# A gated recurrence and a gated convolution on one core: loads per 1024-token chunk, squares of both channel halves together, and a new order of all queues

## Chip, cores and metric

The kernel runs on one core of one Trainium2 chip. The metric is the device time of one execution in microseconds. The engines are TensorE (PE in the profile, its weight loads PEld), VectorE (DVE), ScalarE (ACT) and GpSimd (POOL); SyncE (SP) only issues transfers.

## What is computed

Two layers in a row, for x, r_gate and i_gate of 4 x 6336 x 256 (batch, time, channel), all float32:

```
a    = exp(8 * sigmoid(r_gate) * log(clip(sigmoid(a_param))))
u    = sqrt(max(1 - a*a, 1e-6)) * sigmoid(i_gate) * x
y[t] = a[t] * y[t-1] + u[t]                         # along time, from 0 in each batch
gate = sigmoid(sum over k of conv_w[k] * y[t-4+k])  # causal, 5 taps, per channel
out  = (gate * (y @ w_val)) @ w_out
```

## The kernel before

The 25344 tokens lie in one row. They are cut into 28 chunks: 0 and 1 of 256 tokens, 2 of 512, 3 to 25 of 1024, 26 of 512 and 27 of 256. A chunk of 1024 consists of two windows of 512; there are 51 windows. The 256 channels are two halves h of 128.

The order is written out by hand in ORDER, a string of words such as `ex.5.0` or `cv.7@0,1` (name, chunk or window, half, PSUM banks). The words are emitted in that order, and each engine works through its own words strictly in sequence, waiting for what its next word needs. The steps:

- `lr`, `li`, `lx` (L292, SP): load a window of r, i or x; each partition gets J consecutive tokens of 256 channels (J = 4: 4 KB). The rings have four window slots each; a load waits until the engine that read the slot's old content is done.
- `ta`, `tb` (L310, L313, ScalarE): tanh of half the r and i gates of a whole chunk (sigmoid = half of one plus tanh), to bf16.
- `tr` (L357, TensorE): transposes of the r side, so that channels lie on partitions; `ex` (L378, ScalarE): Exp to a, in the order of time. From chunk 3 on most `tr`/`ex` cover two neighbouring chunks (GROUPS), so `ex.3.0` covers chunks 3 and 4.
- `sq` (L386, GpSimd): a*a per chunk and half; `sa` (L394) is the same on ScalarE, used for two of them (sa.25.1 and sa.27.1).
- `rt` (L405, ScalarE): square roots of 1 - a*a for one of 12 batches of chunks (BATCHES: [0], [1], [2], [3, 4], [5, 6, 7], ..., [23, 24, 25], [26, 27]), to bf16. Sqrt and Exp/Tanh are in different tables of ScalarE; where the next word needs the other table, a table load (L562) is put in.
- `pp` (L320, GpSimd): one plus tanh; `up` (L332, GpSimd): times x, giving the input of a window with bf16 channels laid in pairs of tokens. For windows 1, 2 and 6 `xp` and `uv` (L337, L346) do it on TensorE and VectorE.
- `nt` (L420, TensorE): the roots of a chunk back to tokens on partitions, as pairs of bf16 read as float32; `xg` (L450, VectorE): roots times input; `xt` (L461, TensorE): that product to channels on partitions. For chunks 26 and 27 the order is turned round (L435, L446).
- `sc` (L483, VectorE): the recurrence along time for one half of a chunk.
- `cv` (L495, TensorE): the convolution of a window as 20 small matmuls; `tg` (L502, ScalarE): its tanh; `vl` (L510, TensorE): y @ w_val; `gv` (L515, VectorE): gate times value.
- `ou` (L525, TensorE): times w_out; `cd` (L533, VectorE) or `ca` (L535, ScalarE): copy out of PSUM; `st` (L546, SP): store of the window.
- `wm` (L364): groups of five matmuls on TensorE whose result is not used.
- `s_kt` computes khf, the scale of Exp, from a_param through small operations on TensorE (L233), VectorE (L234 to L248) and ScalarE (L237); `s_diag` makes the matrices of the convolution, `s_wl` and `s_wcast` load and cast the weights.

Of the kernel before, what the change touches and what calls it, by code (L numbers as in the profile page):

```python
# [9 lines left out]
P = 128  # L10
# [14 lines left out]
NU = 8  # L25
# [13 lines left out]
s_ident s_small s_kt s_diag lr.2 lr.0 s_wl.3 lr.1 li.0 lr.3 s_wl.2 ta.2 ta.0 lr.4 tr.0.1@0 tr.2.0@1 lr.6 ta.1 lr.5  # L39
tr.1.0@2 tb.0 tr.0.0@3 li.1 tr.2.1@4 ex.2.0 li.2 tr.1.1@5 li.3 ex.1.1 lx.0 ex.0.1 sq.1.1 li.4 ex.1.0 sq.2.0 ex.0.0  # L40
ex.2.1 sq.1.0 ta.3 sq.2.1 pp.0 sq.0.0 sq.0.1 ta.4 tb.1 lr.10 tr.3.0@4,5 tb.2 lr.9 lr.8 lr.7 lx.2 tr.3.1@2,3 ex.3.0
s_wl.1 up.0 lx.1 lx.4 wm.10@6 ex.3.1 sq.3.0 wm.5@6 lx.3 wm.3@6 tb.3 sq.3.1 wm.9@6 wm.6@6 ta.6 pp.4 sq.4.1 ta.5 lr.13
li.5 xp.2@2,3 li.6 sq.4.0 li.7 lr.14 tr.5.0@4,5 lx.6 uv.2 pp.3 rt.0 rt.2 nt.0@0 up.4 xg.0 rt.1 xt.0@0,1 xp.1@2 rt.3
sc.0.0 nt.1@3 up.3 lx.5 nt.2@0 uv.1 s_wl.0 xg.1 xg.2 xt.1@2,3 sc.0.1 lx.7 sc.1.0 nt.3@6,7 lr.12 sc.1.1 xg.3 ex.5.0
xt.2@0,1 sc.2.1 sc.2.0 tb.4 cv.0@2,3 tr.5.1@4,5 xt.3@6,7 lr.11 li.8 sq.5.0 ex.5.1 tg.0 sc.3.0 pp.5 sc.3.1 cv.2@0,1
s_wcast cv.1@4,5 ta.8 xp.6@2,3 uv.6 vl.0@6,7 tg.1 tg.2 vl.2@0,1 up.5 ta.7 sq.6.1 lx.8 li.9 li.10 lr.17 lr.18
nt.4@2,3 gv.0 tb.5 tr.7.0@6,7 ou.0.0@4 gv.2 ex.7.0 xg.4 sq.6.0 cd.0.0 tr.7.1@0,1 sq.5.1 vl.1@2,3 ou.2.0@4,5 ex.7.1
gv.1 xt.4@6,7 ou.1.0@2 lx.9 li.12 cv.4@0,1 cd.2.0 cv.3@4,5 pp.7 sq.7.1 tb.6 pp.8 sq.7.0 tg.4 tg.3 rt.4 sc.4.1 st.0
sc.4.0 li.11 lr.15 lr.16 st.2 up.7 pp.9 li.14 li.13 vl.3@0,1 vl.4@4,5 gv.3 gv.4 cd.1.0 ou.3.0@0,1 pp.10 up.8 sq.8.1
# [57 lines left out]
def kernel(  # L107
# [82 lines left out]
    with tc.manual_schedule():  # L190
# [403 lines left out]
```

## Time and profile before

| | |
|---|---|
| median of three runs | 287.52 us (287.51 to 288.32) |
| span of the profiled execution | 286.4 us |
| what the median has beyond that span | 1.1 us |
| transfers | 104.76 MB, mean 366 GB/s |
| granted TensorE clock | 0.999 of full speed |

The profiled execution's own whole time is not listed apart from its span. A row of an engine's group reads: line, engine, operation, output and inputs with partitions x elements, count, busy time in us and mean ns of one, and the idle time before them with what ended it. A row of the timeline begins with its start and its length in us; a bracket gives the idle time before it. A row of the chain has a start and a length.

### The profile page before, as it was taken

To read this page: it belongs to the slowest core of one execution; us is meant where nothing else is said; L and a number is where in the kernel's file an instruction comes from. 1 tells how busy PE (TensorE), PEld (TensorE's weight loads), DVE (VectorE), ACT (ScalarE), POOL (GpSimd) and SP (SyncE) were. 2 spreads that over 40 slices of the span, in tenths; PEclk is the share of its full clock that TensorE was granted. 3 is DMA by queue.
4 is the path that set the end of the run, shared out by engine and by line. 5 is a ranking of instruction groups with operands and counts; after the bars stand their busy time and mean duration, and the time that the engine had idled before them with its cause. 6 is when DMAs were issued, how large, how long until landed. Compare 5 with 4: busy or idle time off the path is not lost.

```text
span 286.4 us, 6382 instructions
## 1 busy us (share of the span) xinstructions
PE 251.8 (88%) x2552; PEld 171.1 (60%) x2576; DVE 246.8 (86%) x214; ACT 273.6 (96%) x198; POOL 241.6 (84%) x161
## 2 busy tenths in 40 slices
PE   1387778899999999988988999989989899999993
PEld 1253447456656767455756676656646774767562
DVE  4002898969999899999999999999999999999991
ACT  5999999999999999999999999999999999898984
POOL 1659589899999999999999999999996999874600
PEclk9999999999999999999999999999999999999999
DMA  7999999999999999999999999999999999994536
GB/s 243 384 373 407 409 403 408 388 366 376 410 408 366 418 367 392 414 410 334 405 364 413 411 332 356 420 416 419 415 401 333 359 416 406 364 356 170 192 150 256
DMA packets 29996, 104.76 MB, mean 366 GB/s; under 512 B 3335, under 2 KB 3854, under 8 KB 29966
## 3 DMA queue, kind: packets, MB, share of 16 engines
q1 hardware_dynamic: 29952, 104.35, 94.5%
q8 instruction: 20, 0.33, 0.5%
q14 instruction: 10, 0.08, 0.1%
q10 hardware_dynamic: 14, 0.01, 0.0%
HBM read 78.39 MB, written 25.95 MB: 364 GB/s over the span
## 4 chain that ended last, share of the span: by engine, by line
ACT 33%; PE 29%; DVE 14%; issue 12%; DMA 8%; SPq 1%; ACTq 0%; DVEq 0%
ACT ering L405 8%; PE banks L495 8%; DVE yring L483 7%; PE banks L525 7%; DMA rring<-in_r_gate_dram 6%; ACT tgring L502 6%; ACT taring L310 5%; ACT tbring L313 5%; ACT aring L378 5%; PE banks L510 5%; PE banks L461 3%; DVE tgring L515 3%; PE banks L420 3%; ACT L562 3%; DVE oring L533 2%
## 5 line engine op out<-in xcount | busy, mean ns | idle before, releaser
L386 POOL TENSOR_TENSOR ering<-aring 128x1024 f32<-128x1024 f32 (+2 forms) x54 | 91.5, 1714 | 16.7 <-ACT aring L378 16.4
L332 POOL TENSOR_TENSOR uring<-tbring,xring 128x1024 bf16<-128x1024 bf16 (+1 forms) x48 | 101.1, 2119 | 3.6 <-DMA xring<-in_x_dram 3.1
L483 DVE TENSOR_TENSOR_SCAN yring<-aring,yring,banks 128x1024 bf16<-128x1024 f32 (+5 forms) x50 | 101.7, 2064 | 2.1 <-PE banks L461 1.9
L495 PE MATMUL banks<-yring,diag 64*64 64x512 bf16 (+7 forms) x1080 | 62.1, 361 | 2.3 <-ACT aring L378 1.6
L515 DVE SCALAR_TENSOR_TENSOR tgring<-tgring,banks 128x1024 bf16<-128x1024 bf16 (+1 forms) x51 | 59.1, 1178 | 4.0 <-PE banks L510 3.4
L320 POOL TENSOR_SCALAR tbring<-tbring 128x1024 bf16<-128x1024 bf16 (+1 forms) x48 | 49.1, 1032 | 6.8 <-ACT tbring L313 6.7
L378 ACT ACTIVATE aring<-banks,khf 128x2048 f32<-128x2048 bf16 (+3 forms) x38 | 54.2, 1476 | 0.4 <-PE banks L357 0.3
L525 PE MATMUL banks<-wo,tgring 128*128 128x256 bf16 x396 | 51.0, 274 | 3.7 <-DVE tgring L515 3.2
L502 ACT ACTIVATE tgring<-banks 128x1024 bf16<-128x1024 f32 (+1 forms) x51 | 50.2, 1011 | 2.0 <-PE banks L495 1.9
L510 PE MATMUL banks<-yring,wv 128*128 128x512 bf16 (+4 forms) x192 | 48.1, 359 | 3.7 <-ACT tgring L502 1.9
L310 ACT ACTIVATE taring<-rring 128x2048 bf16<-128x2048 f32 (+2 forms) x28 | 47.9, 1718 | 1.4 <-DMA rring<-in_r_gate_dram 1.4
L525 PEld LDWEIGHTS <-tgring 128*128 128x128 bf16 x396 | 41.2, 114 | 13.1 <-DVE tgring L515 8.8
L313 ACT ACTIVATE tbring<-iring 128x2048 bf16<-128x2048 f32 (+2 forms) x28 | 48.2, 1726 | 0.0
L405 ACT ACTIVATE ering<-ering 128x4096 bf16<-128x4096 f32 (+5 forms) x16 | 44.8, 2840 | 0.1
L495 PEld LDWEIGHTS <-diag 64*64 64x64 bf16 x1080 | 29.0, 106 | 25.6 <-issue 9.9
L533 DVE COPY oring<-banks 128x1024 f32<-128x1024 f32 (+1 forms) x36 | 41.9, 1182 | 1.4 <-PE banks L525 0.7
L357 PE MATMUL banks<-ident_b,taring 128*128 128x128 bf16 x396 | 29.9, 230 | 9.4 <-ACT taring L310 6.7
L357 PEld LDWEIGHTS <-taring 128*128 128x128 bf16 x396 | 26.5, 103 | 14.2 <-ACT taring L310 7.4
L510 PEld LDWEIGHTS <-wv 128*128 128x128 bf16 x216 | 19.7, 98 | 24.5 <-issue 10.3
L450 DVE TENSOR_TENSOR uring<-banks,uring 128x2048 bf16<-128x2048 bf16 (+2 forms) x26 | 29.4, 1134 | 3.5 <-PE banks L420 3.2
L420 PE MATMUL banks<-ident,ering 128*128 128x128 f32 x192 | 28.3, 289 | 1.1 <-ACT ering L405 0.9
L461 PE MATMUL banks<-ident,uring 128*128 128x128 f32 x192 | 25.9, 276 | 3.5 <-DVE uring L450 2.8
(49 smaller groups left out, 154.0 us busy)
## 6 DMA issues: line engine op xcount, KB each, us to landing
rring<-in_r_gate_dram SPq DMA_DIRECT2D x48, 512.0 KB, 8.2
iring<-in_i_gate_dram SPq DMA_DIRECT2D x48, 512.0 KB, 8.7
xring<-in_x_dram SPq DMA_DIRECT2D x48, 512.0 KB, 8.2
out_dram<-oring SPq DMA_DIRECT2D x48, 512.0 KB, 6.5
rring<-in_r_gate_dram SPq DMA_DIRECT2D x3, 256.0 KB, 4.1
iring<-in_i_gate_dram SPq DMA_DIRECT2D x3, 256.0 KB, 6.5
xring<-in_x_dram SPq DMA_DIRECT2D x3, 256.0 KB, 8.5
out_dram<-oring SPq DMA_DIRECT2D x3, 256.0 KB, 5.2
```

The source lines that it names most:

```text
L310: nc.scalar.activation(**tangent(c, taring, NTR, rring, NRI))
L313: nc.scalar.activation(**tangent(c, tbring, NTI, iring, NII))
L332: nc.gpsimd.tensor_tensor(out=u, in0=t1, in1=xt, op=ALU.mult)
L378: nc.scalar.activation(out=dst, in_=src, func=ACT.Exp, scale=khf[:, h:h + 1], bias=khf[:, h:h + 1])
L386: nc.gpsimd.tensor_tensor(out=e, in0=a, in1=a, op=ALU.mult)
L405: nc.scalar.activation(out=ering[:].bitcast(BF16)[:, 4 * o:4 * o + 2 * n], in_=ering[:, 2 * o:2 * o + 2 * n], func=ACT.Sqrt, scale=-0.25, ...
L483: nc.vector.tensor_tensor_scan(out=yring[:, h, col:col + o1 - o0], data0=aring[:, h, a_at[c] + o0:a_at[c] + o1], data1=xT[:, o0:o1], initi ...
L495: nc.tensor.matmul(out=gp[oh * 64:oh * 64 + 64, h, a:b], lhsT=diag[half * 64:half * 64 + 64, h, k, :], rhs=yring[half * 64:half * 64 + 64, ...
L502: nc.scalar.activation(out=tgring[:, w % NTG, :, 0:wins[w]], in_=live.pop(("gp", w))[:, :, 0:wins[w]], func=ACT.Tanh, scale=0.5)
L510: nc.tensor.matmul(out=val[:, m, a:b], lhsT=wv[:, hk, m * P:(m + 1) * P], rhs=yring[:, hk, col:col + b - a], start=(hk == 0), stop=(hk == ...
L515: nc.vector.scalar_tensor_tensor(out=tgring[:, w % NTG, :, 0:wins[w]], in0=tgring[:, w % NTG, :, 0:wins[w]], scalar=1.0, in1=live.pop(("va ...
L525: nc.tensor.matmul(out=ops[:, j * D:(j + 1) * D], lhsT=gv[:, hk, j:wins[w]:J], rhs=wo[:, hk, :], start=(hk == 0), stop=(hk == H - 1))
```

## The change

- ORDER is written anew for all engines. CHUNKS, BATCHES and GROUPS hold the same numbers as before.
- `lr`, `li` and `lx` load a whole chunk: one transfer of 1 MB for 1024 tokens, in which each partition gets eight consecutive tokens (8 KB). There are 28 loads of each kind instead of 51. x goes to slots numbered like those of the gates. Since partition p now holds tokens 8p to 8p + 7 of the chunk, `tr`, `ex`, `nt` and `xt` take steps over the chunk instead of over the window.
- `sq.c` without a half squares both halves of a chunk in one operation; chunks 0, 1, 2, 26 and 27 still have one per half. `sa`, and `sv`, which was not used, are gone.
- The bank of `s_kt` and `s_diag` is given in ORDER.
- Counted in ORDER: `sq` 54 to 33, `sa` 2 to 0, `ca` 15 to 17, `cd` 36 to 34, `wm` 17 to 10, loads 153 to 84. All other words have the same count. Changes between the Sqrt table and the other, 18 to 20.

The core of the diff:

```diff
-s_ident s_small s_kt s_diag lr.2 lr.0 s_wl.3 lr.1 li.0 lr.3 s_wl.2 ta.2 ta.0 lr.4 tr.0.1@0 tr.2.0@1 lr.6 ta.1 lr.5
-tr.1.0@2 tb.0 tr.0.0@3 li.1 tr.2.1@4 ex.2.0 li.2 tr.1.1@5 li.3 ex.1.1 lx.0 ex.0.1 sq.1.1 li.4 ex.1.0 sq.2.0 ex.0.0
-ex.2.1 sq.1.0 ta.3 sq.2.1 pp.0 sq.0.0 sq.0.1 ta.4 tb.1 lr.10 tr.3.0@4,5 tb.2 lr.9 lr.8 lr.7 lx.2 tr.3.1@2,3 ex.3.0
-s_wl.1 up.0 lx.1 lx.4 wm.10@6 ex.3.1 sq.3.0 wm.5@6 lx.3 wm.3@6 tb.3 sq.3.1 wm.9@6 wm.6@6 ta.6 pp.4 sq.4.1 ta.5 lr.13
-li.5 xp.2@2,3 li.6 sq.4.0 li.7 lr.14 tr.5.0@4,5 lx.6 uv.2 pp.3 rt.0 rt.2 nt.0@0 up.4 xg.0 rt.1 xt.0@0,1 xp.1@2 rt.3
...
-cv.41@0,1 st.33 gv.38 vl.37@6,7 lx.45 lr.50 st.35 cd.36.0 lx.46 ou.38.0@2,3 gv.37 li.47 rt.10 cv.40@4,5 tg.41
-ou.37.0@6,7 cd.38.0 nt.23@2,3 up.43 li.48 lr.49 st.36 cd.37.0 vl.41@6,7 xg.23 vl.40@0,1 up.45 gv.41 st.34 tg.40
-nt.24@2,3 xt.23@6,7 gv.40 up.46 xg.24 ou.39.0@0,1 cv.42@2,3 sc.23.0 ou.41.0@4,5 sc.23.1 tb.25 ca.39.0 ou.40.0@0,1
...
+s_ident lr.0 lr.2 lr.1 s_small li.1 ta.0 tr.0.1@5 tr.0.0@3 s_kt@0 wm.5@2 lr.3 s_wl.3 lx.1 li.0 ta.2 ta.1 tb.1 lx.0
+ex.0.1 li.2 lr.4 tr.2.1@2 tr.2.0@0 ex.2.0 tr.1.0@1 ex.1.0 tr.1.1@4 ex.2.1 ta.3 ex.1.1 ex.0.0 tb.0 sq.1.0 sq.2.1 sq.0.1
+sq.1.1 sq.0.0 xp.1@5 s_wl.2 lr.5 pp.0 sq.2.0 rt.0 rt.1 nt.0@6 nt.1@4 rt.2 lx.2 s_wl.1 s_wl.0 up.0 uv.1 xg.0 xt.0@3,0
+ta.4 xg.1 xt.1@2,1 tb.2 lr.6 tr.3.1@6,7 sc.0.0 ta.5 sc.0.1 sc.1.1 li.4 li.3 lx.3 s_diag@4 s_wcast ex.3.1 nt.2@5
+xp.2@0,1 uv.2 tr.3.0@3,4 ex.3.0 xg.2 xt.2@0,6 sc.1.0 cv.1@1,2 ta.6 sq.3 sq.4 cv.0@4,5 tg.0 sc.2.0 sc.2.1 vl.2@6,7
+cv.2@4,5 tg.1 tb.4 tg.2 tr.5.1@0,1 lr.8 lx.4 lr.7 vl.0@2,3 gv.0 tb.3 tr.5.0@4,5 gv.2 ou.0.0@7 ou.2.0@2,3 cd.0.0 cd.2.0
+ex.5.0 li.5 vl.1@2,3 li.6 rt.3 pp.5 pp.3 gv.1 up.3 pp.4 xp.6@2,3 uv.6 ou.1.0@4 cd.1.0 up.4 up.5 nt.3@6,7 xg.3 ta.8
+ex.5.1 sq.6 sq.5 nt.4@2,3 xg.4 xt.3@6,5 xt.4@7,4 wm.1@0 wm.8@1 ta.7 tr.7.1@2,3 st.0 st.2 st.1 lr.10 lx.5 lr.9 sc.3.1
+tb.5 ex.7.1 tr.7.0@0,1 sc.3.0 ex.7.0 cv.3@5,6 sc.4.1 sc.4.0 pp.8 sq.7 pp.7 cv.4@2,3 tg.4 tg.3 tb.6 vl.4@0,1 vl.3@6,7
+gv.3 gv.4 up.7 pp.9 up.8 ou.3.0@6,7 rt.4 cd.3.0 wm.6@3 ou.4.0@0,1 wm.3@2 vl.6@4,5 cv.6@2,3 lx.6 li.7 tg.6 st.3 li.8
...
+sc.21.0 tg.38 tr.25.0@0 ex.25.0 cv.37@5,6 tg.37 tr.25.1@3 ex.25.1 ou.36.0@0,1 xt.22@6,2 sc.21.1 cv.39@4,5 sc.22.1
+sc.22.0 vl.38@2,3 gv.38 pp.43 sq.25 tb.24 tg.39 ca.36.0 vl.37@4,5 rt.10 vl.39@6,7 cv.40@0,1 gv.39 gv.37 ou.38.0@2,3
+cv.41@6,7 cd.38.0 pp.45 pp.44 ou.37.0@4,5 cd.37.0 up.44 up.43 nt.23@2,3 xg.23 tg.40 li.26 st.36 st.33 li.27 lx.25
+st.37 st.38 vl.40@4,5 gv.40 tg.41 ta.26 vl.41@0,1 gv.41 ou.39.0@2,3 ca.39.0 tb.25 up.45 pp.46 up.46 xt.23@6,7 sc.23.0
...
-        def s_kt():
-            kps = banks[:, 0]
+        def s_kt(at):
+            kps = banks[:, at]
...
-        def load(w, which):
-            n = wins[w]
-            J = n // P
-            if which == "x":
-                dst = xring[:, w % NX, 0:J, :]
-            else:
-                ring = rring if which == "r" else iring
-                dst = ring[:, place(w, NRI if which == "r" else NII), 0:J, :]
-            nc.sync.dma_start(dst, flat[which][wstart[w]:wstart[w] + n, :].rearrange("(p j) d -> p j d", p=P))
-
-        def op_lr(w):
-            load(w, "r")
-
-        def op_li(w):
-            load(w, "i")
-
-        def op_lx(w):
-            load(w, "x")
+        def load(c, which):
+            w, k, n = cwins[c][0], len(cwins[c]), clen[c]
+            ring, slots = {"r": (rring, NRI), "i": (iring, NII), "x": (xring, NX)}[which]
+            at = place(w, slots)
+            dst = ring[:, at:at + k, 0:wins[w] // P, :].rearrange("p w j d -> p (w j) d")
+            nc.sync.dma_start(dst, flat[which][cstart[c]:cstart[c] + n, :].rearrange("(p j) d -> p j d", p=P))
+
+        def op_lr(c):
+            load(c, "r")
+
+        def op_li(c):
+            load(c, "i")
+
+        def op_lx(c):
+            load(c, "x")
...
         def op_tr(c, h, *at):
-            ws = [w for k in sorted(group_of[c], key=lambda k: a_at[k]) for w in cwins[k]]
-            J = wins[ws[0]] // P
+            cs = sorted(group_of[c], key=lambda k: a_at[k])
+            J = wins[cwins[c][0]] // P
             bank = banks[:, at[0]:at[-1] + 1].rearrange("c k n -> c (k n)").bitcast(BF16)
-            for g, w in enumerate(ws):
-                assert wins[w] == J * P
-                for j in range(J):
-                    o = (j * len(ws) + g) * P
-                    nc.tensor.transpose(out=bank[:, o:o + P],
-                                        in_=taring[:, place(w, NTR), j, h * P:(h + 1) * P],
-                                        identity=ident_b[:])
+            for g, k in enumerate(cs):
+                for v, w in enumerate(cwins[k]):
+                    assert wins[w] == J * P and len(cwins[k]) == len(cwins[c])
+                    for j in range(J):
+                        o = ((v * J + j) * len(cs) + g) * P
+                        nc.tensor.transpose(out=bank[:, o:o + P],
+                                            in_=taring[:, place(w, NTR), j, h * P:(h + 1) * P],
+                                            identity=ident_b[:])
             live["rT", c, h] = bank
...
-            J = wins[cwins[c][0]] // P
+            J = n // P
...
-        def op_sq(c, h):
-            e, a = squares(c, h)
+        def both_squares(c):
+            n = clen[c]
+            return (ering[:, H * e_at[c]:H * (e_at[c] + n)].rearrange("p (h n) -> p h n", h=H),
+                    aring[:, :, a_at[c]:a_at[c] + n])
+
+        def op_sq(c, *h):
+            e, a = squares(c, h[0]) if h else both_squares(c)
             nc.gpsimd.tensor_tensor(out=e, in0=a, in1=a, op=ALU.mult)
-
-        def op_sv(c, h):
-            e, a = squares(c, h)
-            nc.vector.tensor_tensor(out=e, in0=a, in1=a, op=ALU.mult)
-
-        def op_sa(c, h):
-            e, a = squares(c, h)
-            nc.scalar.activation(out=e, in_=a, func=ACT.Square)
 
...
         def op_nt(c, *at):
             bank = banks[:, at[0]:at[-1] + 1].rearrange("p b n -> p (b n)")
-            k = 0
-            for w in cwins[c]:
-                nq = wins[w] // (2 * P)
-                o = live["n", c] + (wstart[w] - cstart[c]) // 2
-                for q in range(nq):
-                    for h in range(H):
-                        e = o + h * clen[c] // 2
-                        nc.tensor.transpose(out=bank[:, k:k + P], in_=ering[:, e + q:e + wins[w] // 2:nq], identity=ident[:])
-                        k += P
+            k, n = 0, clen[c]
+            nq = n // (2 * P)
+            for q in range(nq):
+                for h in range(H):
+                    e = live["n", c] + h * n // 2
+                    nc.tensor.transpose(out=bank[:, k:k + P], in_=ering[:, e + q:e + n // 2:nq], identity=ident[:])
+                    k += P
             live["nT", c] = bank[:, 0:k]
...
+        def pairs(c):
+            return [(uring[:, (w + 1) % NU, q], v * (wins[w] // (2 * P)) + q)
+                    for v, w in enumerate(cwins[c]) for q in range(wins[w] // (2 * P))]
...
+            nq = clen[c] // (2 * P)
             for h in range(H):
                 bank = banks[:, at[h]]
-                for w in cwins[c]:
-                    nq = wins[w] // (2 * P)
-                    o = (wstart[w] - cstart[c]) // 2
-                    for q in range(nq):
-                        nc.tensor.transpose(
-                            out=bank[:, o + q:o + wins[w] // 2:nq],
-                            in_=uring[:, (w + 1) % NU, q, h * P:(h + 1) * P, :].rearrange("p d two -> p (d two)")
-                            .bitcast(FP32),
-                            identity=ident[:])
+                for u, q in pairs(c):
+                    nc.tensor.transpose(
+                        out=bank[:, q:clen[c] // 2:nq],
+                        in_=u[:, h * P:(h + 1) * P, :].rearrange("p d two -> p (d two)").bitcast(FP32),
+                        identity=ident[:])
                 live["xT", c, h] = bank
```

More of the change, by code (lines that the diff above doesn't have):

```diff
@@ L44 @@
[L44 to L48, printed above, removed]
@@ L327, in u_args @@
             return (uring[:, (w + 1) % NU, 0:wins[w] // (2 * P)].rearrange("p q d two -> p q two d"),
-                    by_pair(tbring[:, place(w, NTI)], w), by_pair(xring[:, w % NX], w))
+                    by_pair(tbring[:, place(w, NTI)], w), by_pair(xring[:, place(w, NX)], w))
         def op_up(w):
@@ L337, in op_xp @@
                 nc.tensor.matmul(out=ps[:, q], lhsT=ident[:],
-                                 rhs=xring[:, w % NX, 2 * q:2 * q + 2, :].rearrange("p two d -> p (two d)"),
+                                 rhs=xring[:, place(w, NX), 2 * q:2 * q + 2, :].rearrange("p two d -> p (two d)"),
                                  start=True, stop=True)
```

121 lines of the change are left out of this document (55 added, 66 removed).

## Prediction

> **What bounds the kernel now.** I read the page first, for its span and the engines' shares; then the busy time by stage; then the chain of waits, to see which engine ends each stage; then single rows for prices.
>
> ```profile
> span 286.4 us, 6382 instructions
> PE 251.8 (88%) x2552; PEld 171.1 (60%) x2576; DVE 246.8 (86%) x214; ACT 273.6 (96%) x198; POOL 241.6 (84%) x161
> ```
>
> ```profile
> 30.00:40.00 10.00, 7.48 (x87) 5.33 (x86) 9.39 (x11) 9.97 (x5) 5.77 (x5) 1.00 1.03 403
> 60.00:80.00 20.00, 18.96 (x182) 12.53 (x186) 17.89 (x13) 19.97 (x13) 20.00 (x12) 1.00 1.00 382
> 120.00:140.00 20.00, 18.01 (x172) 12.53 (x166) 19.62 (x16) 19.97 (x11) 20.00 (x13) 1.00 1.01 380
> 180.00:200.00 20.00, 18.85 (x197) 12.80 (x196) 19.80 (x16) 19.96 (x15) 19.92 (x13) 1.00 1.03 418
> 240.00:260.00 20.00, 19.56 (x183) 13.45 (x185) 19.68 (x16) 17.56 (x16) 15.53 (x10) 1.00 0.98 359
> ```
>
> A window row gives, after its length, the busy time of PE, weight loads, DVE, ACT and POOL, then granted clock, DMA share and GB/s. Every engine is nearly full, but from 30 to 240 us only ScalarE never pauses: 19.96 to 19.97 of 20. After 240 it has pauses (17.56) while TensorE is at 19.56. So there are three stages: a start, a middle that lasts as long as ScalarE's work, and a tail. The chain shows where the tail begins:
>
> ```profile
> 238.87 5.34 ACT ering L405
> 244.25 1.24 PE banks L420 x8
> 255.37 1.21 PE banks L495 x20
> 256.57 0.97 PE banks L510 x4
> 257.54 0.95 PE banks L420 x8
> 260.89 0.87 PE banks L525 x8
> 261.76 0.87 PE banks L461 x8
> 282.17 0.63 PE banks L525 x4
> 282.82 0.58 ACT oring L535
> ```
>
> The square roots of batch 10 (rt.10, L405) end at 244.2; nt.23 starts at once, and from there the chain is almost all TensorE up to 282.80. Then come the last copy and the store: 42.2 us from the end of rt.10 to the end of the span.
>
> So the sum has three terms: how much ScalarE work stands in its queue up to rt.10, how long ScalarE idles before it, and whether the 42.2 us change.
>
> **1. ScalarE's queue up to rt.10.** I count both orders. Each has 26 ta, 25 tb, 34 ex, 40 tg and 11 rt up to there, of the same sizes. Three things differ. The new order runs rt.0, rt.1 and rt.2 early, goes back to ta.4, and runs rt.3 later by itself: 18 table switches become 20, both new ones early. Copies on ScalarE (ca) up to there are 3 before and 5 after. The square sa.25.1 goes to GpSimd.
>
> ```profile
> 229.97 1.12 ACT L394 ACTIVATE ering<-aring 128x1024 f32<-128x1024 f32 x1
> 230.92 1.98 ACT L313 ACTIVATE tbring<-iring 128x2048 bf16<-128x2048 f32 x1
> 237.57 1.28 ACT L562 ACT_TABLE_LOAD   x1
> 238.87 5.33 ACT L405 ACTIVATE ering<-ering 128x6144 bf16<-128x6144 f32 x1
> 253.02 1.92 ACT L535 COPY oring<-banks 128x1024 f32<-128x1024 f32 x2
> 254.81 0.59 ACT L378 ACTIVATE aring<-banks,khf 128x256 f32<-128x256 bf16 x1
> ```
>
> From start to next start, a table load takes 1.30 us, a copy 0.90 (1.79 for two), the square 0.95. The term is 2 x 1.30 + 2 x 0.90 - 0.95 = **+3.5 us**. Nothing hides it, for ScalarE has no gap in the middle. The Exp (L378) now writes eight tokens per row instead of four, with the same element count, contiguous output and the same kind of stepped input: I take 0.
>
> **2. ScalarE's idle time at the start.**
>
> ```profile
> 0.71 1.28 ACT L191 ACT_TABLE_LOAD   x1 [0.71 <-PEq L578]
> 3.85 0.20 ACT L237 ACTIVATE ktmp<-ktmp 128x2 f32<-128x2 f32 x1 [1.85 <-DVE ktmp L236]
> 4.54 1.58 ACT L310 ACTIVATE taring<-rring 128x1024 bf16<-128x1024 f32 x2 [0.49 <-DMA rring<-in_r_gate_dram]
> 6.35 0.63 ACT L310 ACTIVATE taring<-rring 128x512 bf16<-128x512 f32 x1 [0.23 <-DMA rring<-in_r_gate_dram]
> 13.40 1.91 ACT L310 ACTIVATE taring<-rring 128x2048 bf16<-128x2048 f32 x1 [0.38 <-DMA rring<-in_r_gate_dram]
> ```
>
> ```profile
> 3.46 0.16 DVE L234 COPY ksig<-banks 128x2 f32<-128x2 f32 x1 [3.46 <-PE banks L233]
> ```
>
> The brackets give the wait before each row: 3.7 us so far, and a few smaller pauses follow. In the new order lr.0 (256 KB) leaves alone at the head, where ta.2 and ta.0 needed 768 KB. Half a megabyte at the 403 GB/s above is 1.3 us, so ta.0 starts between 3.2 and 4.5; I take 3.8. But the transposes of s_kt now stand behind tr.0 on TensorE, which waits for ta.0 (0.6 us): VectorE's copy of ksig moves from 3.46 to some 4.8, and with it all small operations up to khf. ScalarE waits some 0.85 for the Exp of s_kt and 0.75 for khf. That makes 0.7 + 1.8 + 0.85 + 0.75 = 4.1 us against 3.7 and the smaller pauses: I take **+0.2**. Bounds: -1.8, if only the first load is waited for, at its earliest; +1.5, if the whole megabyte of chunk 3, which must land before ta.3, is late by about its second half.
>
> Early square roots need early squares:
>
> ```profile
> L386 POOL TENSOR_TENSOR ering<-aring 128x1024 f32<-128x1024 f32 x45 | 84.4, 1896 | 6.1 <-ACT aring L378 5.8
> L386 POOL TENSOR_TENSOR ering<-aring 128x512 f32<-128x512 f32 x4 | 4.2, 1039 | 2.9 <-ACT aring L378 2.9
> L386 POOL TENSOR_TENSOR ering<-aring 128x256 f32<-128x256 f32 x5 | 3.0, 613 | 7.6 <-ACT aring L378 7.6
> L332 POOL TENSOR_TENSOR uring<-tbring,xring 128x1024 bf16<-128x1024 bf16 x46 | 98.7, 2161 | 0.3
> ```
>
> After the last Exp of chunk 0, GpSimd has at most two squares of 0.61 us before rt.0; ScalarE has tb.0 (0.63, as its twin L310 above) and the table load of 1.30: no wait. Doubling 512 elements adds 0.86 us, so 0.18 us is fixed and an operation of 2 x 1024 takes about 3.6 us: 22 merged pairs save GpSimd 22 x 0.18 = 4 us, and the two squares that come from ScalarE (1.9 and 0.6) give over half of it back. GpSimd isn't the bound: 0. The merged square now waits for the second Exp as well, and the pp and up behind it in GpSimd's queue wait with it. Before rt.10, ScalarE has 5.3 us of other work (tb.24, tg.39, ca.36, the table load) after ex.25.1, GpSimd at most 3.6 + 1.05 (pp.43): it fits by 0.7 us. If it doesn't, ScalarE waits; that is a rival below.
>
> **3. The transfers.** 153 loads become 84; pieces of 4 KB become 8 KB.
>
> ```profile
> q1 hardware_dynamic: 29952, 104.35, 94.5%
> ```
>
> ```profile
> SPq L292 <- ACT tbring L313: 26.2, 11, 5.0
> SPq L292 <- POOL uring L332: 19.9, 13, 4.6
> ```
>
> The issuing queue waits mostly for buffers that ScalarE and GpSimd still read, not for transfers, and ScalarE has no wait on a load in the middle. A faster transfer lands in time that is hidden: 0, whether the pieces stay whole or are cut again. On SP a load of x now waits for both products of the old chunk, up to 2.16 us longer than for one; the gate loads, stores and next x behind it wait too. GpSimd's slack of a few us covers it; else the rival below.
>
> **4. The tail.** From nt.23 on both orders hold the same TensorE work: 9 convolutions (L495), 11 value products (L510), 12 output products (L525), 3 nt, 5 xt, 4 tr. At the chain's prices of 1.21, 0.97, 0.87, 0.95 and 0.87 for full ones, and as much less for smaller ones, this is some 37.7 us of the 38.5 from 244.25 to 282.80. VectorE too has the same list from xg.23 on. Three more TensorE products and two gate products now stand between rt.10's place and nt.23; they run beside the 6.6 us of table load and square roots. Left: the operands' steps. nt now takes every fourth pair of tokens, so its weight loads step 4 words instead of 2.
>
> ```profile
> L420 PEld LDWEIGHTS banks<-ident,ering x192: 140/209/223, 28.5 to 258.1; 128*128 128x128 f32 x192
> L461 PEld LDWEIGHTS banks<-ident,uring x192: 137/141/152, 29.6 to 262.3; 128*128 128x128 f32 x192
> ```
>
> Min/median/max: step 1 loads in 140 ns, step 2 in 209. Yet eight nt cost 0.95 us against 0.87 for eight xt (step 1): most of the longer load hides under the matmul before it. Another doubling costs from 0 to 0.95 us per chunk (twice the spacing); by the nearest row, 0.08 to 0.3. For the three chunks in the tail I take **+0.6**. TensorE also loses 7 of 17 filler groups, all before the tail: 0, since it isn't the bound there.
>
> ```profile
> 92.12 1.08 PE banks L364 x5
> ```
>
> The Trainium skill, "SBUF — State Buffer", Specifications, says that SBUF reads in lines of 16 bytes and wants at least two hits in a line for full bandwidth; step 4 leaves one. Here step 2, with two hits, is already slower than step 1, which that sentence doesn't say, and no row has one hit. By the rule the load would fall to half rate, which is the second case below.
>
> **The sum.** 286.4 + 3.5 + 0.2 + 0.6 = 290.7 us of span. The median of the three runs, 287.52, lies 1.1 above the profiled span, so 291.8.
>
> **Rivals.**
> Stepped weight loads pace TensorE: nt takes 0.95 us more per chunk, so the tail is 2.9 longer instead of 0.6, and in the middle TensorE (18.9 of 20, less 0.6 for fillers, plus 1.9 for two chunks) fills up and costs ScalarE 1 to 2 us: 295.5. For it: the jump from 140 to 209. Against: the 0.08 us which that jump cost.
> Coarser waits reach ScalarE: the merged squares or the megabyte of x come too late for the square roots, 0.5 to 1 us in each of 8 batches: 297. For it: a margin of 0.7 us. Against: GpSimd's work is some 2 us less.
> VectorE paces the middle (it is at 19.6 to 19.8 of 20):
>
> ```profile
> 29.94 0.69 DVE L483 TENSOR_TENSOR_SCAN yring<-aring,banks 128x256 bf16<-128x256 f32 x1 [0.41 <-PE banks L461]
> L533 DVE COPY oring<-banks 128x1024 f32<-128x1024 f32 x34 | 40.6, 1212 | 1.4 <-PE banks L525 0.7 <-issue 0.4
> ```
>
> Its first scan then starts near 18 instead of 29.94, but after chunks 0 to 2 it waits for rt.3 near 42, so that lead is gone; two copies of 1.21 us leave it: 284.0 + 1.1 = 285.1, faster. It decides if ScalarE has 3.5 us to spare between 30 and 240; the windows show 0.03 us in 20.
> Nothing visible: ScalarE's start at its bound (-1.8) and a tail without the 0.8 us that aren't products: 286.4 + 3.5 - 1.8 - 0.8 + 1.1 = 288.4, just at the edge of 0.3%.
>
> **Chances.** Forecast 0.58; stepped loads 0.16; coarse waits 0.11; VectorE, faster, 0.08; nothing visible 0.07. A measurement of this kernel tells 0.3% (0.9 us) from no change. Faster 0.08, within 0.3% 0.07, slower 0.85. The range takes in the bounds of start and tail and both slower rivals: 288.6 to 297.0; outside stay the faster case, most of the same one and the end of the coarse waits.
>
> **What would show it.** 20 table loads, 17 ScalarE copies, no L394; ScalarE again without a gap in the middle; the last but one group of square roots ending near 248; 42 to 43 us after it. Weight loads of nt above 209 ns, squares of 2 x 1024 near 3.6 us, about 19,200 packets instead of 29,952 (25 chunks x 3 x 128 fewer pieces, 16 fewer for each of 69 loads). I am wrong if ScalarE idles in the middle, if the tail is shorter than 40 us, or if the new table loads fall into a pause.

## The result, and the profile after

| | before | after |
|---|---|---|
| median | 287.92 us (287.51 to 288.46, 4 runs) | 307.47 us (305.90 to 309.87, 4 runs) |
| span of the profiled execution | 286.4 us | 306.2 us (whole time 308.25) |

The ratio is 1.069, 95% interval 1.064 to 1.074: 19.6 us slower, where 4.3 had been forecast. The page of the changed kernel, in the rows that answer to those shown before:

```profile
span 306.2 us, 6179 instructions
PE 254.9 (83%) x2541; PEld 172.1 (56%) x2541; DVE 245.8 (80%) x212; ACT 277.3 (91%) x200; POOL 242.0 (79%) x140
q1 hardware_dynamic: 20016, 104.34, 87.5%
```

ScalarE is busy 3.7 us longer, as the forecast's first term has it, but the span grew by 19.8. ScalarE's idle time went from 12.8 us (286.4 - 273.6) to 28.9 (306.2 - 277.3): 16.1 us more. The stretches show where (length; busy PE, weight loads, DVE, ACT, POOL; granted clock, DMA share, GB/s):

```profile
40.00:60.00 20.00, 13.89 (x124) 8.97 (x125) 13.89 (x10) 16.30 (x9) 14.14 (x8) 0.97 1.01 419
100.00:120.00 20.00, 14.72 (x168) 10.51 (x168) 16.31 (x15) 13.88 (x12) 16.88 (x9) 0.92 0.82 336
180.00:200.00 20.00, 18.71 (x221) 12.87 (x223) 20.00 (x15) 19.97 (x14) 20.00 (x11) 1.00 0.99 377
240.00:260.00 20.00, 15.59 (x172) 10.13 (x174) 15.48 (x10) 16.27 (x12) 17.50 (x9) 0.91 1.02 421
```

Between 180 and 200 us all is as before: ScalarE 19.97 of 20. In the other three it has a hole of 3.7 to 6.1 us. ScalarE's timeline names the waits (start, length, instruction; in brackets the idle time before it and what ended it), and its last row is rt.10:

```profile
55.55 4.01 ACT L369 ACTIVATE aring<-banks,khf 128x2048 f32<-128x2048 bf16 x2 [3.67 <-POOL ering L382]
116.28 1.20 ACT L369 ACTIVATE aring<-banks,khf 128x1024 f32<-128x1024 bf16 x1 [6.10 <-POOL ering L382]
248.77 1.20 ACT L369 ACTIVATE aring<-banks,khf 128x1024 f32<-128x1024 bf16 x1 [2.76 <-POOL ering L382]
257.96 5.33 ACT L393 ACTIVATE ering<-ering 128x6144 bf16<-128x6144 f32 x1
```

L369 is an Exp (`ex`), L382 a square (`sq`). Three times an Exp waits for a square, 12.5 us in all; the kernel before has no such wait. rt.10 ends at 263.3 instead of 244.2, 19.1 us later, and from there it is 42.9 us to the end instead of 42.2. GpSimd's timeline has the squares that the Exps wait for, each ending 0.03 us before its Exp starts:

```profile
48.36 7.16 POOL L382 TENSOR_TENSOR ering<-aring 128x2048 f32<-128x2048 f32 x2 [2.67 <-ACT aring L369]
112.65 3.60 POOL L382 TENSOR_TENSOR ering<-aring 128x2048 f32<-128x2048 f32 x1
241.58 7.16 POOL L382 TENSOR_TENSOR ering<-aring 128x2048 f32<-128x2048 f32 x2
```

By their place in ORDER they are sq.6 and sq.5 ahead of ex.7.1, sq.12 ahead of ex.11.0, and sq.24 and sq.23 ahead of ex.25.0.

**Why should an Exp wait for another chunk's square?** aring is laid out as [half][5120 columns], five slots of 1024 columns in each half. ex.7.1 writes columns 0 to 2047 of half 1; sq.6 reads columns 4096 to 5119 of both halves: no column in common. But from the first to the last column that sq.6 touches, half 0 column 4096 to half 1 column 5119, lies all of half 1 up to there, with the columns of ex.7.1. The same holds for sq.5 (3072 to 4095), which ends last, for sq.12 (column 0 of half 0 to column 1023 of half 1, so all of half 0) with ex.11.0 (half 0, 4096 to 5119), and for sq.24 and sq.23 (2048 to 3071 and 1024 to 2047) with ex.25.0 (half 0, 3072 to 4095). That gives **theory A**: the merged square counts as a reader of its whole range, and waits are put in for columns that it never reads (false waits). Its rivals: **theory B**, one operation of 3.60 us that needs both halves and frees both late is what costs; and a third, that order and whole-chunk loads cost it, and the squares are only where it shows.

### The profile page after: what moved, and what is told of

It reads as the page before. It is cut to its first block, busy times and chain, and to the rows that moved or that the text cites. A ratio compares the mean times of both kernels' runs of the same rounds, so it can differ in the third digit from the quotient of the medians.

```text
span 306.2 us, 6179 instructions
## 1 busy us (share of the span) xinstructions
PE 254.9 (83%) x2541; PEld 172.1 (56%) x2541; DVE 245.8 (80%) x212; ACT 277.3 (91%) x200; POOL 242.0 (79%) x140
## 3 DMA queue, kind: packets, MB, share of 16 engines
q1 hardware_dynamic: 20016, 104.34, 87.5%
## 5 line engine op out<-in xcount | busy, mean ns | idle before, releaser
L382 POOL TENSOR_TENSOR ering<-aring 128x2048 f32<-128x2048 f32 (+2 forms) x33 | 90.3, 2747 | 26.7 <-ACT aring L369 26.5
L479 PE MATMUL banks<-yring,diag 64*64 64x512 bf16 (+7 forms) x1080 | 64.3, 368 | 9.7 <-ACT aring L369 8.0
L369 ACT ACTIVATE aring<-banks,khf 128x2048 f32<-128x2048 bf16 (+3 forms) x38 | 54.7, 1470 | 15.7 <-POOL ering L382 12.5
L509 PE MATMUL banks<-wo,tgring 128*128 128x256 bf16 x396 | 52.1, 277 | 7.1 <-ACT aring L369 3.4
L494 PE MATMUL banks<-yring,wv 128*128 128x512 bf16 (+4 forms) x216 | 51.2, 371 | 8.0 <-DVE yring L467 2.6
L479 PEld LDWEIGHTS <-diag 64*64 64x64 bf16 x1080 | 30.4, 108 | 34.6 <-issue 18.8
L517 DVE COPY oring<-banks 128x1024 f32<-128x1024 f32 (+1 forms) x34 | 39.8, 1186 | 3.7 <-PE banks L509 3.0
L494 PEld LDWEIGHTS <-wv 128*128 128x128 bf16 x216 | 20.9, 100 | 30.0 <-issue 15.6
L348 PE MATMUL banks<-ident_b,taring 128*128 128x128 bf16 x396 | 29.4, 228 | 7.8 <-ACT taring L300 5.5
L348 PEld LDWEIGHTS <-taring 128*128 128x128 bf16 x396 | 25.9, 102 | 14.2 <-issue 6.1
L406 PE MATMUL banks<-ident,ering 128*128 128x128 f32 x192 | 28.9, 295 | 4.1 <-ACT ering L393 3.2
L446 PE MATMUL banks<-ident,uring 128*128 128x128 f32 x192 | 27.1, 285 | 4.6 <-DVE uring L437 3.8
```

Source lines behind the costliest of these rows:

```text
L348: nc.tensor.transpose(out=bank[:, o:o + P], in_=taring[:, place(w, NTR), j, h * P:(h + 1) * P], identity=ident_b[:])
L369: nc.scalar.activation(out=dst, in_=src, func=ACT.Exp, scale=khf[:, h:h + 1], bias=khf[:, h:h + 1])
L382: nc.gpsimd.tensor_tensor(out=e, in0=a, in1=a, op=ALU.mult)
L479: nc.tensor.matmul(out=gp[oh * 64:oh * 64 + 64, h, a:b], lhsT=diag[half * 64:half * 64 + 64, h, k, :], rhs=yring[half * 64:half * 64 + 64, ...
L494: nc.tensor.matmul(out=val[:, m, a:b], lhsT=wv[:, hk, m * P:(m + 1) * P], rhs=yring[:, hk, col:col + b - a], start=(hk == 0), stop=(hk == ...
L509: nc.tensor.matmul(out=ops[:, j * D:(j + 1) * D], lhsT=gv[:, hk, j:wins[w]:J], rhs=wo[:, hk, :], start=(hk == 0), stop=(hk == H - 1))
```

## The experiments

All medians are compared with the kernel before on the same chip (287.55 to 287.76 us); intervals are 95%. Where no ratio is given there was one run.

### Which part of the change costs what

**order_only**: the new order, but with the old loads per window and the old squares.

```diff
-... lr.5 ... sq.3 ...
+... lr.7 lr.8 ... sq.3.0 sq.3.1 ...      (all else as in the new ORDER, code as before)
```

> The new order with window loads of 512 KB (two in the place of each new one) and squares per half, so neither of the other two parts. The step of the forecast that stands: 3.5 us more ScalarE work, 291 to 293. The changed kernel with split squares took 295.6; if its whole-chunk loads are not to blame, this one takes 294.5 to 297 as well, and the rest above the forecast is the order's own waits.

Measured 293.60 us, ratio 1.021 (1.016 to 1.026); span 290.8. This is its rt.10: it ends at 248.2, 4.0 us later than before, and from there it is 42.6 us to the end:

```profile
242.88 5.33 ACT L342 ACTIVATE ering<-ering 128x6144 bf16<-128x6144 f32 x1
```

The median lies between the two expected ranges. The forecast's span was 290.7, and this profiled run, the fastest of the four, has it; the median is 1.8 us above the forecast's 291.8.

**split_half**: the changed kernel with each merged square issued as two, one per half.

```diff
-            e, a = squares(c, h[0]) if h else both_squares(c)
-            nc.gpsimd.tensor_tensor(out=e, in0=a, in1=a, op=ALU.mult)
+            for k in (h or range(H)):
+                e, a = squares(c, k)
+                nc.gpsimd.tensor_tensor(out=e, in0=a, in1=a, op=ALU.mult)
```

> The changed kernel with each merged square issued as two operations, one per channel half, at the same place of GpSimd's queue. Theory A: the merged square names one stretch from the start of its columns in half 0 to their end in half 1, so an Exp into columns that it never reads waits for it; ScalarE's three waits for GpSimd (12.5 us) come from that. Then they go, and the time falls to 292 (the forecast without them) to 296. Theory B: the order and the loads of a whole chunk are late by themselves; GpSimd has 4 us more work than in the changed kernel and the time stays at 303 to 310.

Measured 295.64 us, ratio 1.029 (1.026 to 1.032), in theory A's range. No Exp waits for a square any more; the longest wait for one stands ahead of square roots, where the forecast had seen a risk, and is small:

```profile
123.89 5.33 ACT L394 ACTIVATE ering<-ering 128x6144 bf16<-128x6144 f32 x1 [1.01 <-POOL ering L383]
```

So the 19.6 us come apart: order 6.0 (293.60 - 287.6), whole-chunk loads 2.0 (295.64 - 293.60), merged squares 11.8 (307.47 - 295.64); they add to 19.8, since the kernel before had 287.9 beside the changed kernel and 287.6 beside these two. The first two are known to some 1.5 us, by the interval of order_only. The third rival is out for the 11.8 us; order and loads cost some 8 by themselves.

**loads_only**: the old order and squares per half, all loads by whole chunk, each at the later of the two old places of its windows.

```diff
-... lx.7 ... lx.8 ...
+... lx.5 ...             (likewise lr, li; load, tr, ex, nt, xt as in the changed kernel)
```

> The old order with one part of the change alone: whole-chunk loads (1 MB, 8 KB pieces) in the place of the later of the two window loads, and the token steps in the transposes that follow from them; squares per half as before. If transfers are hidden and the longer step of the weight loads costs nothing, as the changed kernel's rows say: within 1.5 us of the kernel before, 286 to 289. If coarser buffers are what costs: 291 to 300, with ScalarE or GpSimd waiting on x or on the gates.

Measured 296.31 us, ratio 1.029 (1.026 to 1.033): 8.8 us, as the theory of coarser buffers had it, and more than in the new order. GpSimd's waits (total, times, longest), and what they make ScalarE wait for:

```profile
POOL uring L266 <- DMA xring<-in_x_dram: 16.8, 9, 4.0
```

```profile
72.64 1.91 ACT L247 ACTIVATE tbring<-iring 128x2048 bf16<-128x2048 f32 x1 [1.54 <-POOL uring L266]
80.75 1.91 ACT L247 ACTIVATE tbring<-iring 128x2048 bf16<-128x2048 f32 x1 [1.07 <-POOL uring L266]
177.67 1.91 ACT L247 ACTIVATE tbring<-iring 128x2048 bf16<-128x2048 f32 x1 [0.92 <-POOL uring L266]
```

The products of x with the input gate (L266) wait nine times for x, where the kernel before has one such wait of 3.1 us, and then the gate tanh (L247) waits until those products free its ring.

**x_window**: loads_only, but x per window again, at its old places.

```diff
+        def op_lx(w):
...
+            part = flat["x"][cstart[c]:cstart[c] + clen[c], :].rearrange("(p v j) d -> p v j d", p=P, v=k)
+            nc.sync.dma_start(xring[:, place(w, NX), 0:J, :], part[:, v])
```

> Old order, squares per half, gates r and i loaded by whole chunks (1 MB, 8 KB pieces) at the later of the two old places, but x loaded per window as before (512 KB in 4 KB pieces) at its old places. Only x's transfers differ from loads_only (296.31 us against 287.55 for the kernel before). Theory A, the 8.8 us of loads_only come from x: a buffer of x is free only when GpSimd has done both products of a chunk, so the load goes out one window late and GpSimd waits for it: 287 to 289.5 us, and GpSimd's products wait for loads of x about 3 us in all, as in the kernel before. Theory B, the whole-chunk gate loads or transfers of 1 MB as such cost it: 292 to 297 us.

Measured 289.76 us, ratio 1.006 (1.005 to 1.008): a little above theory A's range, far below B's. The waits for x are gone:

```profile
POOL uring L269 <- DMA xring<-in_x_dram: 2.5, 2, 2.2
```

Some 6.5 of the 8.8 us come from x: with two chunk slots in its ring, a load can start only when the second product of a chunk is done, while a window slot is free one product earlier; and the first product now waits for the whole megabyte. These runs don't part the two. The transfers themselves are no slower: the queue's time is 94.5% of 286.4 = 270.6 us before, and here

```profile
q1 hardware_dynamic: 23328, 104.34, 93.5%
```

of 286.7 = 268.1 us, with 22% fewer packets.

### Why the merged squares cost 12 us

**before_merged**: the kernel before with merged squares (chunks 3 to 24) at the later of their two places, nothing else.

```diff
-... sq.7.1 ... sq.7.0 ...
+... sq.7 ...              (op_sq as in the changed kernel)
```

> The kernel before with one part of the change alone: the squares of both halves of chunks 3 to 24 as one operation, at the place of the later of the two in the old order. Theory A: ScalarE gets waits for GpSimd that it did not have, 292 to 303. Theory B: within 2 us of the kernel before, 286 to 290, since GpSimd has 4 us less work and no other queue changes.

Measured 306.13 us, one run: 18.6 us, more than either theory had. Here GpSimd itself waits longer for Exps, and ScalarE then for GpSimd's products; before it was 16.4 us in 7 waits, and none:

```profile
POOL ering L328 <- ACT aring L315: 32.0, 11, 7.8
ACT tbring L250 <- POOL uring L269: 6.7, 2, 6.1
```

Ahead of an Exp ScalarE waits for a square only 1.9 us in all. A false wait would work in both directions, but these runs don't divide the 18.6 us.

**split_cols**: the changed kernel with each merged square cut into two of 512 columns, both over both halves.

```diff
...
+            for k in range(2):
+                nc.gpsimd.tensor_tensor(out=e[:, :, k * n:k * n + n], in0=a[:, :, k * n:k * n + n],
+                                        in1=a[:, :, k * n:k * n + n], op=ALU.mult)       # n = clen[c] // 2
```

> The changed kernel with each merged square as two operations of 2 x 512 columns, both spanning both halves. Control: the same number and size of operations as with the split by half. Theory A: the stretch named is nearly as wide, the waits stay at 9 to 13 us, time 303 to 311. If smaller operations were what helps, it would be 291 to 297.

Measured 300.23 us, one run: between the two ranges. ScalarE's waits for squares ahead of an Exp are 4.6 us in all, where theory A had 9 to 13. The first stall is still there, though the operation is half as long:

```profile
55.50 4.01 ACT L369 ACTIVATE aring<-banks,khf 128x2048 f32<-128x2048 bf16 x2 [3.96 <-POOL ering L388]
```

The other two are gone, though the range of the halved squares still takes in the columns of both Exps. In ORDER both stand behind their squares. Yet ex.11.0, the second in the first row, has run before sq.12, which the second row begins with, and ex.25.0 (third row) starts while sq.23, the later half of the fourth row, is under way:

```profile
110.75 2.31 ACT L369 ACTIVATE aring<-banks,khf 128x1024 f32<-128x1024 bf16 x2
115.05 7.46 POOL L388 TENSOR_TENSOR ering<-aring 128x1024 f32<-128x1024 f32 x4
242.16 1.20 ACT L369 ACTIVATE aring<-banks,khf 128x1024 f32<-128x1024 bf16 x1
237.71 7.45 POOL L388 TENSOR_TENSOR ering<-aring 128x1024 f32<-128x1024 f32 x4
```

Here the Exp and each halved square touch 1024 columns. ex.7.1, which still waits, writes 2048; and in the changed kernel every merged square reads 2048. So theory A is too wide as it was put: in these runs the range counted only where one of the two operations touches 2048 columns. What sets that border, and what puts the waits in, no run shows.

**flat**: merged squares, aring laid out chunk by chunk (half 0, then half 1), so that a merged square covers unbroken columns.

```diff
-            return ering[:, at:at + clen[c]], aring[:, h, a_at[c]:a_at[c] + clen[c]]
+            o = H * a_at[c] + h * clen[c]
+            return ering[:, at:at + clen[c]], aring[:, o:o + clen[c]]
...
```

> The changed kernel with both halves of a chunk side by side in aring (chunk, half, time), so that the merged square reads one stretch without a gap; squares stay merged, queues are the same. Theory A: the three waits go here too, 290 to 296, and 0 to 3 us under the split squares, which have 4 us more GpSimd work. Theory B: 303 to 310. If it were the length of one merged operation that holds ScalarE, this kernel would stay slow and the split one be fast.

Measured 299.99 us, ratio 1.044 (1.042 to 1.046): between the theories. No Exp waits for a square, but an Exp of two chunks now leaps over the other half and has such a range itself. It waits for a scan (L468):

```profile
55.73 2.06 ACT L370 ACTIVATE aring<-banks,khf 128x2048 f32<-128x2048 bf16 x1 [2.48 <-DVE yring L468]
```

**grouped** and **old_grouped**: halves side by side for each pair of chunks that one Exp writes.

```diff
...
+            at, m = min(a_at[k] for k in g), sum(clen[k] for k in g)
...
+            return H * at + h * m + a_at[c] - at
...
```

> The changed kernel with its merged squares, but aring laid out so that the chunks that one Exp writes lie together: for each such group first half 0 of its chunks, then half 1. An Exp still writes one unbroken run of columns, and the range from a merged square's first to its last column stays inside its own group. Same operations, same order, same lengths as the changed kernel. Theory A, the cost of merging is false waits for columns that merely lie inside the range of a square: 293.5 to 296.5 us (per-half squares gave 295.64), and ScalarE waits for no square ahead of an Exp. Theory B, merging costs because one operation of 3.60 us needs both halves and releases both late: 300 to 307 us, as in the changed kernel (307.47).

> The kernel before, in the old order and with its loads per window, with merged squares at the later of the two old places (as in before_merged, 306.13 us) and the same grouped layout of aring. Theory A, false waits: 287 to 291 us, within 1 per cent of the kernel before (287.73), and no wait of ScalarE for GpSimd above 1 us. Theory B, the long operation and its need of both halves: 298 to 306 us.

Measured 304.65 us (ratio 1.059, 1.055 to 1.063) and 301.01 us (1.044, 1.041 to 1.048). Both lie in theory B's range, though ScalarE waits for no square ahead of an Exp in either. Neither tells: in this layout ex.7 writes over half 0 of chunk 4 before its scan has read it, so these kernels compute other values, and Exps and scans wait for each other where they didn't before (a row of old_grouped):

```profile
ACT aring L319 <- DVE yring L435: 8.0, 3, 4.7
```

**ex_half, ex_merged, ex_flat**: so the Exp of a pair was issued as one operation per chunk in all three. ex_half is split_half with that edit, ex_merged the changed kernel, ex_flat the flat layout. Now no operation of ex_flat leaps over foreign columns.

```diff
-            nc.scalar.activation(out=dst, in_=src, func=ACT.Exp, scale=khf[:, h:h + 1], bias=khf[:, h:h + 1])
+            for i, a in enumerate(at):
+                dst = aring[:, h, a:a + n]          # ex_flat: aring[:, H * a + h * n:H * a + h * n + n]
+                nc.scalar.activation(out=dst.rearrange("c (q j) -> c q j", j=J), in_=src[:, i], func=ACT.Exp, ...)
```

> Control. The changed kernel with squares per half (as split_half, 295.64 us) and every Exp of a pair of chunks issued as two operations, one per chunk; layout of aring as in the changed kernel. 9 pairs x 2 halves add 18 operations on ScalarE, each two of 1.20 us for one of 2.01: up to 7 us of work more. Both theories expect the same here, 297 to 303 us; the other two kernels are read against it.

> The changed kernel, merged squares over both halves in the old layout (a range that spans other chunks' columns), with one Exp per chunk as in ex_half. Both theories expect 6 to 13 us more than ex_half, with waits of ScalarE for squares ahead of an Exp.

> Merged squares and one Exp per chunk as in ex_merged, but aring laid out chunk by chunk, half 0 and half 1 of a chunk side by side, so that a merged square and an Exp each cover one unbroken run of columns and no range spans another chunk's. Theory A, false waits: as ex_half within 1 per cent, at best 2 us less because GpSimd saves 22 x 0.18 us, and no wait of ScalarE for a square ahead of an Exp. Theory B, the long operation that needs both halves and releases both late: as ex_merged, 6 to 13 us above ex_half.

| | median | ratio to before (95%) | span | longest wait of an Exp for a square |
|---|---|---|---|---|
| ex_half | 298.39 us | 1.037 (1.034 to 1.040) | 295.3 | none |
| ex_merged | 312.49 us | 1.085 (1.083 to 1.087) | 312.6 | 5.78 us |
| ex_flat | 298.65 us | 1.039 (1.035 to 1.043) | 295.3 | none |

The spans are of single runs: the slowest of ex_merged's four, the fastest of the others'. The squares in the two merged kernels are the same operations with the same length (first row ex_merged, second ex_flat; count, then busy us and mean ns):

```profile
L380 POOL TENSOR_TENSOR ering<-aring 128x2048 f32<-128x2048 f32 (+2 forms) x33 | 90.3, 2751 | 30.3 <-ACT aring L366 30.3
```

```profile
L380 POOL TENSOR_TENSOR ering<-aring 128x2048 f32<-128x2048 f32 (+2 forms) x33 | 90.2, 2749 | 19.4 <-ACT aring L366 19.4
```

Only where the columns lie differs, and it is worth 13.8 us, all of the cost of merging within the noise (ex_merged is 14.1 us above ex_half, where 6 to 13 had been expected). ex_merged has three stalls ahead of an Exp again; in ex_flat the first entry of ScalarE's waits is for TensorE (first fence ex_merged, second ex_flat):

```profile
57.94 4.49 ACT L366 ACTIVATE aring<-banks,khf 128x1024 f32<-128x1024 bf16 x4 [3.67 <-POOL ering L380]
119.70 1.21 ACT L366 ACTIVATE aring<-banks,khf 128x1024 f32<-128x1024 bf16 x1 [5.78 <-POOL ering L380]
254.76 1.21 ACT L366 ACTIVATE aring<-banks,khf 128x1024 f32<-128x1024 bf16 x1 [1.63 <-POOL ering L380]
```

```profile
ACT aring L366 <- PE banks L348: 3.4, 4, 1.2
```

Theory A stands, theory B falls: needing both halves in one operation of 3.60 us costs nothing that can be measured here (298.65 against 298.39). It saves nothing either: GpSimd waits 19.4 us for Exps in ex_flat anyway.

Nor does a merged square hold up every Exp into aring. In the changed kernel sq.14 (2048 to 3071 of both halves) and ex.15.1 (half 1, 3072 to 5119), by their place in ORDER, run at the same time, for ex.15.1 lies behind the last column of sq.14:

```profile
149.77 3.60 POOL L382 TENSOR_TENSOR ering<-aring 128x2048 f32<-128x2048 f32 x1
151.38 2.07 ACT L369 ACTIVATE aring<-banks,khf 128x2048 f32<-128x2048 bf16 x1
```

### Does ScalarE's work set the length?

**more_tables**: the kernel before with four table loads more. **light_sq** and **light**: the kernel before with less work on ScalarE.

```diff
-... tg.9 ... tg.27 ...                              more_tables (xl: one load of each table)
+... tg.9 xl ... tg.27 xl ...
-... ca.19.0 ... ca.23.0 ... ca.33.0 ... sa.25.1     light (light_sq: only the last)
+... cd.19.0 ... cd.23.0 ... cd.33.0 ... sq.25.1
```

> The kernel before, with two extra pairs of activation table loads on ScalarE (square-root set and back to the exponential set), one behind tg.9 and one behind tg.27: 4 loads at 1.30 us, no other edit. Theory A, the first term of the forecast, ScalarE's work up to rt.10 sets the length one to one: 287.5 + 5.2 = 292.7 us, within 0.8. Theory B, another engine paces the middle or slack takes it up: 287.5 to 290 us. Theory C, a late ScalarE costs more than its own work, because what it hands to the others comes late too: 294 us or more.

> The kernel before with the square sa.25.1 on GpSimd instead of ScalarE, nothing else. Theory A, ScalarE's queue sets it: 0.95 us less, 286.6 us. Theory B, rt.10 waits for GpSimd, which has 1.90 us more to do just ahead of it: 287.5 to 289 us.

> The kernel before with less work on ScalarE up to rt.10: the square sa.25.1 on GpSimd and the copies of windows 19, 23 and 33 on VectorE, at the same places of the order. Theory A, ScalarE alone paces: 0.95 + 3 x 0.90 = 3.65 us less, 283.9 us. Theory B, VectorE (three copies of 1.21 us more) or GpSimd (one square of 1.90 us more before rt.10) takes over at once: 286.5 to 290 us.

more_tables: 294.47 us, ratio 1.022 (1.019 to 1.025): 6.7 us for 5.2 us of work, above A and in C's range. At rt.10 it is 6.5 (245.34 against 238.87), and one wait is new, a tanh whose convolution comes late:

```profile
197.80 1.02 ACT L506 ACTIVATE tgring<-banks 128x1024 bf16<-128x1024 f32 x1 [0.99 <-PE banks L499]
245.34 5.33 ACT L409 ACTIVATE ering<-ering 128x6144 bf16<-128x6144 f32 x1
```

light_sq: 289.07 us, ratio 1.004 (1.002 to 1.006), at the upper end of theory B, but not for its reason: rt.10 waits for no square and starts at 238.66, 0.2 us earlier than before. The 0.95 us that ScalarE saves go mostly into a new wait of 0.97 us for TensorE just ahead of it, and from rt.10 to the end it is 43.3 us instead of 42.2. light: 294.73 us, ratio 1.023 (1.020 to 1.026), above both. Less work on ScalarE made the kernel **slower**, light by 7 us. VectorE is busy 250.3 us there, and ScalarE now waits in the middle for transposes of TensorE, which wait for a bank that VectorE's copies free late (a stretch of light, with ScalarE at 35.17 of 40 us; then the transposes of nt on TensorE and an Exp on ScalarE):

```profile
140.00:180.00 40.00, 34.82 (x408) 25.35 (x404) 38.68 (x32) 35.17 (x22) 36.74 (x23) 1.00 0.95 362
```

```profile
154.69 1.20 PE L420 MATMUL banks<-ident,ering 128*128 128x128 f32 x8 [2.19 <-DVE oring L533]
157.69 2.06 ACT L378 ACTIVATE aring<-banks,khf 128x2048 f32<-128x2048 bf16 x1 [2.08 <-PE banks L357]
```

So work added to ScalarE counts in full and somewhat more; work taken from it and given to GpSimd gained nothing, and with copies given to VectorE too it cost 7 us. No kernel tried beats the one before.

## Why the prediction was wrong

1. **ScalarE's queue, +3.5 us: right.** 20 table loads of 1283 ns, two copies more, no square; in order_only, where only this and the start act, rt.10 ends 4.0 us later, against 3.5 + 0.2 (its fastest run). That nothing hides such work is borne out by more_tables.
2. **Start, +0.2 us: about right.** Steps 1 and 2 together are 0.3 off. ScalarE's first waits in the changed kernel were forecast at 1.8, 0.85 and 0.75 us:

```profile
3.59 0.63 ACT L300 ACTIVATE taring<-rring 128x512 bf16<-128x512 f32 x1 [1.59 <-DMA rring<-in_r_gate_dram]
5.51 0.20 ACT L230 ACTIVATE ktmp<-ktmp 128x2 f32<-128x2 f32 x1 [1.29 <-DVE ktmp L229]
8.58 2.35 ACT L369 ACTIVATE aring<-banks,khf 128x256 f32<-128x256 bf16 x4 [0.88 <-DVE khf L241]
```

3. **Squares at 0: this step failed**, with 11.8 of the 15.7 us by which the forecast fell short (307.47 - 291.8). It said: "GpSimd isn't the bound: 0. The merged square now waits for the second Exp as well". It asked what the square waits for and who is behind it in GpSimd's queue; of those that wait for the square it weighed the square roots alone, and not a later Exp that writes into aring. No Exp that waited shares a column with its square; but the merged square, with its 2048 columns, counts with the range from its first to its last, and a range over both halves takes in all slots between. The price of the operation, 3.6 us, was exact, and the margin ahead of rt.10 held (the square roots of the changed kernel are idle for 0.1 us in all).
4. **Transfers at 0: off by 2.0 us** in this order. The chunk slots were seen ("up to 2.16 us longer"), and "GpSimd's slack of a few us covers it" held nearly; in the old order it doesn't, and the same edit costs 8.8. Of packets 19,200 were forecast and 20,016 came: the count took 25 chunks of two windows where there are 23. Shorter DMA time was worth nothing, as the step says. The Trainium skill, "DMA: Bandwidth & Descriptors", Bandwidth, says to batch transfers to 1 MiB or more; here the queue's time fell by 1% (267.9 us, 87.5% of 306.2, against 270.6), and the coarser slots cost more than that.
5. **Tail, +0.6 us: size right (0.7), reason wrong.** The weight loads of nt at step 4 take no longer than at step 2 (209 ns in the fence of step 4 of the prediction):

```profile
L406 PEld LDWEIGHTS banks<-ident,ering 128*128 128x128 f32 x192 | 25.3, 208 | 9.3 <-ACT ering L393 4.8 <-issue 1.9 <-DVE tgring L499 0.9
```

order_only, which keeps step 2, already has 0.4 of the 0.7. By the Trainium skill's rule on 16-byte lines, quoted there, this load would have fallen below full bandwidth; half rate was the prediction's reading of it. The measurement, 208 ns against 209, decides against it for this load, and the rival built on it is out. What makes step 2 slower than step 1 stays open.
6. **The rival "coarser waits reach ScalarE"** (297 us) came nearest. It put the waits ahead of the square roots, 0.5 to 1 us in each of 8 batches; they stood ahead of three Exps, 2.8 to 6.1 us each. The sign "I am wrong if ScalarE idles in the middle" is what came.
7. **What remains, 1.8 us.** The span of order_only is the forecast's, but that was its fastest run (292.56 us); its others took up to 295.77, and the median is 293.60 against the 291.8 forecast. What spreads them isn't settled.

## What to carry to other kernels

Before two operations are merged into one that leaps over a gap, take the range from its first to its last element and ask who writes or reads anything inside it: a wait may be put in for each, and if it costs time, lay the parts side by side first, and then look at every other operation on that buffer, as the two-chunk Exp showed. Doubling a load's size in a ring of the same bytes halves its number of slots, so price it by when the slot comes free and not by the transfer. In a kernel with all engines near full, "the bound engine" says what added work costs, not what removed work saves.

## What was not expected of the hardware

The granted TensorE clock falls after pauses of TensorE. In the changed kernel, from 10 to 20 and from 20 to 30 us (the row of 180 to 200 us above has 1.00):

```profile
10.00:20.00 10.00, 5.17 (x18) 2.67 (x18) 2.76 (x6) 9.64 (x12) 6.11 (x8) 0.54 1.02 393
20.00:30.00 10.00, 7.68 (x79) 5.38 (x79) 6.61 (x10) 9.10 (x6) 4.02 (x5) 0.78 0.88 340
```

TensorE's timeline has a pause of 4.18 us just before, and then eight transposes (L348) in 1.06 us; further on sixteen such take as long:

```profile
12.29 2.05 PE L327 MATMUL banks<-xring,ident 128*128 128x512 f32 x2 [4.18 <-DMA xring<-in_x_dram]
18.99 1.06 PE L348 MATMUL banks<-ident_b,taring 128*128 128x128 bf16 x8
25.69 1.06 PE L348 MATMUL banks<-ident_b,taring 128*128 128x128 bf16 x16
```

The three stalls make pauses of 4.02, 3.98 and 2.79 us on TensorE:

```profile
57.66 1.45 PE L479 MATMUL banks<-yring,diag 64*64 64x512 bf16 x20 [4.02 <-ACT aring L369]
250.02 1.87 PE L509 MATMUL banks<-wo,tgring 128*128 128x256 bf16 x8 [2.79 <-ACT aring L369]
```

Behind each the granted clock is 0.50 for some microseconds (60 to 62, 118 to 122 and 250 to 252 us), as it is from 12 to 24 us. So a false wait on ScalarE also slows the matmuls behind it: sixteen transposes take 1.89 us at 119.82 and 1.06 again at 125.42. The Trainium skill, "TensorE: Matmul & The Clock Gate", What's actually happening, says that TensorE falls back to half its clock after an idle window of about 3.4 us. The trace agrees on the half (0.50) and on the three longer pauses; the one of 2.79 us is shorter than that window, and the clock fell there too. What share of the time that has wasn't tried; from 263 to 300 us the clock is back at 1.00.

A slow start isn't new. The kernel before has a pause of 4.49 us too, and eight transposes behind it take as long as sixteen do at 36.80 us (1.05), though its windows there read a clock of 1.00:

```profile
13.08 1.03 PE L357 MATMUL banks<-ident_b,taring 128*128 128x128 bf16 x8 [4.49 <-ACT taring L310]
```

So a 1.00 in a window at the start doesn't show that TensorE ran at full speed.
